# Gate weights spread by one broadcast DMA, strip 0 on ScalarE's queue, tile 3's transposes copied by ScalarE

## The chip, the cores and the metric

The kernel runs on one core of a Trainium2 chip. The metric is the device time of one execution in microseconds (us). The core has five engines with instruction queues of their own: TensorE (PE in the profile, its weight loads PEld), VectorE (DVE), ScalarE (ACT), GpSimd (POOL) and SyncE (SP, which here only issues DMAs). They wait for one another through semaphores. SyncE, ScalarE and GpSimd issue DMAs; all of these are moved by the same 16 DMA engines.

## The reference

Inputs are bfloat16: x of 2048 x 512 (one tensor of the two serves both branches), and weights.

```
g = sigmoid((x * gate_w).sum(-1))                 # one gate for each of the 2048 rows
a = attention(x, wqkv) @ wo                       # 32 heads of 16; each row sees 8 keys: itself and 2, 4, ... 14 rows back
h = layernorm(x)                                  # over the 512 features
u = gelu(h.T @ w1 + b1)                           # mixes the 2048 rows into 1792
y = (u @ w2 + b2).T                               # and back to 2048
out = g * a + (1 - g) * y
```

## The kernel before

All of the input fits in SBUF. x is held as 16 tiles of 128 rows by 512 features. The work is written as a list of operations with their reads, writes and guessed durations; a small planner (class _Sched) orders them for each engine by ready time and remaining path, and then every engine runs its list strictly in that order, with semaphore waits where one engine's operation needs another's. So an operation that waits holds up everything behind it on its engine.

The order on TensorE is: five warm-up products on constants (L568); transposes of x tiles 0 to 3 through PSUM (L586); the transposes of the two bias rows (L602, L603); one product that spreads the gate weights over the partitions (L643); four groups of "lead" products (L618), which begin the first layer of the token mixer for x tiles 0 to 3 as soon as each is normalised; the q, k and v projections (L713, 192 products); the rest of the mixer's first layer (L609), with the two score sums of the attention (L803, one for each half of the rows) put in between; and the second layer (L937) with the output projection of the attention (L946) behind it.

VectorE first takes the statistics of x tiles 0 to 3 (L623 and L627), and normalises each (L634) once ScalarE has made the reciprocal deviation with two small functions. It then computes the gate sums: for each x tile one multiply-and-reduce with the gate weights (L756, 16 in all, the tensor GWB of 128 x 512 holds the gate weights in every partition). Then come the products of queries with shifted keys for the attention (L468), which fill most of its time, with the statistics of the other tiles (L775) in between. The score sum of each half needs VectorE's last addition for that half.

How the gate weights get into GWB before the change: GpSimd clears a tensor of 128 x 512 (GWZ, L478), a DMA on ScalarE's queue puts the 1 KB of gate weights in its partition 0, TensorE multiplies it with a matrix of ones (L643, into PSUM bank 6), and ScalarE copies the product to GWB.

The transposes of x tiles 0 to 3 are copied from PSUM to the tensor XT, which the first projections read: those of tiles 0 to 2 by ScalarE (through the helper at L471), those of tile 3 by VectorE (L598). The bias transposes go to PSUM bank 7, beside tile 3's, and VectorE copies them (L674, L675).

The loads at the start are in a row on SyncE's queue, in the order in which they are written: x0, x1, x2, strip 0, x3, strips 1 to 3 (a strip is the part of w1 that the lead products of one tile use, 128 KB), the K weights in two parts, the first part of the Q weights, x4 and x5, the second Q weights, then transposing loads of x and the rest. ScalarE's queue has the two bias rows and the gate row. A load's operation waits only for its buffer; SyncE needs about 0.47 us for each issue.

Of the kernel before, what the change touches and what calls it, by code (L numbers as in the profile page):

```python
# [5 lines left out]
BF16 = mybir.dt.bfloat16  # L6
# [3 lines left out]
AF = mybir.ActivationFunctionType  # L10
# [3 lines left out]
D = 512  # L14
# [4 lines left out]
NST = S // 128  # L19
NFT = F // 128  # L20
# [8 lines left out]
NLEAD = 4  # L29
AVD = (1, 3, 5, 6)  # L30
GL = 4
# [259 lines left out]
class _Mem:  # L291
# [17 lines left out]
    def view(self, name, dtype, dims, extra=0, p0=0, np_=128):  # L309
        base = self.arena[:].bitcast(dtype)  # L310
        pst = base.ap[0][0]
        esz = mybir.dt.size(dtype)
        o = self.off[name]
        assert o % esz == 0
        return bass.AP(base.tensor, p0 * pst + o // esz + extra, [[pst, np_]] + [list(d) for d in dims])


def bass_gated_mix__sliding_local_dilated__mixer_token_mlp__prompt_kernel(nc, A_x, A_wqkv, A_wo, B_x, B_w1, B_b1, B_w2, B_b2, gate_w, out, dbg=None):
    with contextlib.ExitStack() as es:
# [49 lines left out]
        w1v = B_w1.rearrange("(st p) f -> p st f", p=128)  # L369
# [17 lines left out]
        W2ALIAS = [["w1s2"], ["w1s3"], ["w1s4"], ["p2"], ["w1s0"], ["w1s1"],  # L387
                   ["x%d" % t for t in range(7)], ["x%d" % t for t in range(7, 14)]]
        XTUSE = ["w1s3", "w1s4"]
        PR = [["p0", "p0b"], ["p1", "p1b"], ["p2", "p2h"], ["log0", "log1", "att0", "att1", "lw0", "lw1", "lw2", "lw3", "gwr"]]  # L390
        LW = view("LOG", BF16, [(128 * GL, NLEAD), (1, 128 * GL)])
        WO = view("WO", BF16, [(D, 4), (1, D)])
        QH = [view("Q%d" % h, BF16, [(HS, 4), (1, HS)]) for h in range(2)]
# [4 lines left out]
        LOG = [view("LOG", BF16, [(UT_, NW), (1, UT_)], extra=h * NW * UT_) for h in range(2)]  # L398
# [12 lines left out]
        E32 = view("E32", FP32, [(1, D)])  # L411
        GWB = view("GWB", BF16, [(1, D)])
        LX = view("LX", BF16, [(D, NLEAD), (1, D)])
        GWZ = view("LOG", BF16, [(1, D)], extra=NLEAD * 128 * GL)
        GW1 = psub(GWZ, 0, 1, 0, [(1, D)])
        JUNK = view("S4", BF16, [(D, 4), (1, D)])
        ZN = view("Z", FP32, [(1, 32)])
        TZ = view("Z", FP32, [(1, 32)], extra=32)
# [2 lines left out]
        IDENT = view("IDENT", BF16, [(1, 128)])  # L421
# [4 lines left out]
        B1R = view("ROWS", BF16, [(1, 128)], np_=NFT)  # L426
        B2R = view("ROWS", BF16, [(1, 128)], extra=128, np_=NST)
# [26 lines left out]
        B1C = small(NFT)  # L454
        B2C = small(NST)
# [5 lines left out]
        def psb(bank):  # L461
            return ps[:, bank, :].bitcast(BF16)
# [7 lines left out]
        def act(o_, i_, f_, **kw):  # L470
            return lambda e: e.activation(out=o_, in_=i_, func=f_, **kw)  # L471
# [3 lines left out]
        A("pool", lambda e: e.affine_select(out=IDENT, in_=ONES, pattern=[[1, 128]], compare_op=ALU.is_equal,  # L475
                                            fill=0.0, base=0, channel_multiplier=-1),
          0.4, reads=["ones"], writes=["ident"], name="ident")
        A("pool", lambda e: e.memset(GWZ, 0.0), 0.4, writes=["gwr"], name="gwz", prio=-50)  # L478
        A("pool", lambda e: e.memset(sub(KH[0], 0, [(KR, 4), (1, PAD)]), 0.0), 0.2, writes=["kpad"], name="kpad")  # L479
        A("pool", lambda e: e.memset(sub(V5, 0, [(VR, 4), (1, PAD)]), 0.0), 0.2, writes=["vpad"], name="vpad")  # L480

# [9 lines left out]

        last_ld = [None]

        def load(name, dst, src, nbytes, writes, transpose=False, queue="sp", issue=0.5, order=True, deps=(), reads=()):
            ds = sch.dsem(name)

            def fn(e):
                if transpose:
                    return e.dma_start_transpose(dst, src)
                return e.dma_start(dst, src)  # L500
            op = sch.dma(queue, fn, nbytes, ds, issue=issue, reads=reads, writes=writes, deps=deps,
                         after=([last_ld[0]] if order and last_ld[0] is not None else []), name=name)
            if order:
                last_ld[0] = op
            return op
# [11 lines left out]
        def ld_wq(name, d0, d1, res):  # L517
            load(name, WQKV[:, d0:d1, 0:D], wqkv_v[:, d0:d1, 0:D], (d1 - d0) * 128 * D * 2, [res], queue="act", order=False)

        def ld_strip(t, n):  # L520
            load("s%d" % t, LW[:, t:t + n, :], w1v[:, t:t + n, 0:128 * GL], n * 32768 * GL, ["lw%d" % t_ for t_ in range(t, t + n)])

        ld_x(0, 1)
        ld_x(1, 1)
        ld_x(2, 1)
        ld_strip(0, 1)
        ld_x(3, 1)
        ld_strip(1, 1)
        ld_strip(2, 1)
        ld_strip(3, 1)  # L530
        ld_w("wk01", 1, 0, 2, "wk")
        ld_w("wk23", 1, 2, 4, "wk2")
        load("gw", GW1, bass.AP(gate_w.tensor, gate_w.offset, [[D, 1], [1, D]]), 1024, ["gwr"], issue=0.4, queue="act", order=False)
        load("b1", B1R, B_b1.rearrange("(t p) -> t p", p=128), 4096, ["b1r"], issue=0.4, queue="act", order=False)
        load("b2", B2R, B_b2.rearrange("(t p) -> t p", p=128), 4096, ["b2r"], issue=0.4, queue="act", order=False)
        ld_w("wq01", 0, 0, 2, "wq")
        ld_x(4, 2)
        ld_w("wq23", 0, 2, 4, "wq2")
# [22 lines left out]
        WONE = nc.const_aps.tensor(1.0, [128, 128], BF16)  # L561
        WROW = nc.const_aps.tensor(1.0, [128, 512], BF16)

        def f_warm(n, bank):
# [4 lines left out]
                return ins  # L569
            return fn  # L570

        chain = [None]

        def PE(fn, dur, reads, writes, name, prio=0):
            op = A("pe", fn, dur, reads=reads, writes=writes, after=([chain[0]] if chain[0] is not None else []), name=name, prio=prio)
            chain[0] = op
            return op
# [12 lines left out]
        def tx(t):  # L590
            PE(f_tx(t), 0.4, ["x%d" % t, "ident"], ["b%d" % TXB[t][0]], "tx%d" % t)

        def ext(t, eng, after):
            bank, o = TXB[t]
            src = sub(psb(bank), o, [(128, 4), (1, 128)])
            dst = sub(XT, t * 128, [(S, 4), (1, 128)])
            if eng == "dve":
                return A("dve", lambda e: e.tensor_copy(out=dst, in_=src), 0.42, reads=["b%d" % bank], writes=["xt0_%d" % t], after=after, name="ext%d" % t, prio=-30)  # L598
            return A("act", act(dst, src, AF.Copy), 0.6, reads=["b%d" % bank], writes=["xt0_%d" % t], after=after, name="ext%d" % t, prio=-30)

        def f_tb(e):
            e.transpose(out=psb(7)[:, 512:512 + NFT], in_=B1R, identity=IDENT[0:NFT, 0:NFT])  # L602
            return e.transpose(out=psb(7)[:, 544:544 + NST], in_=B2R, identity=IDENT[0:NST, 0:NST])  # L603

        def f_ph2(ft, bank, s0, s1):
            def fn(e):
# [22 lines left out]
        def rstd(t, after=()):  # L629
            A("act", act(col(SD, t), AG[:, t, 1:2], AF.Ln, bias=1e-5), 0.25, reads=["ag%d" % t], writes=["sd%d" % t], after=after, name="lnl%d" % t, prio=-40)  # L630
            return A("act", act(col(RSTD, t), col(SD, t), AF.Exp, scale=-0.5), 0.25, reads=["sd%d" % t], writes=["rstd%d" % t], name="rs%d" % t, prio=-40)

        def apply(t, after):
            return A("dve", (lambda t_: lambda e: e.tensor_scalar(out=LX[:, t_, :], in0=X[:, t_, :], scalar1=AG[:, t_, 0:1], scalar2=col(RSTD, t_),  # L634
                                                                  op0=ALU.subtract, op1=ALU.mult))(t), 0.41, reads=["rstd%d" % t, "st%d" % t, "x%d" % t],
                     writes=["lx%d" % t], after=after, name="ln%d" % t, prio=-40)

        PE(f_warm(5, 0), 2.1, [], ["b0"], "warm0")
        tx(0)
        tx(1)  # L640
        PE(f_tb, 0.2, ["b1r", "b2r", "ident"], ["b7"], "t_b12")
        tx(2)
        PE(lambda e: e.matmul(ps[:, 6, :], lhsT=WONE, rhs=GWZ, start=True, stop=True), 0.4, ["gwr"], ["b6"], "gwbc")  # L643
        def lead(t):
            PE(f_lead(t), 0.87, ["lx%d" % t, "lw%d" % t], ["b%d" % ft for ft in range(GL)], "lead%d" % t)

# [1 line left out]
        ag = aggr(0)  # L648
# [3 lines left out]
        e0 = ext(0, "act", [r0])  # L652
        lead(0)
        ag = aggr(1, [l0])
        r1 = rstd(1)
        ew = A("act", act(GWB, ps[:, 6, :], AF.Copy), 0.6, reads=["b6"], writes=["gwb"], after=[r1], name="evgw", prio=-50)
        tx(3)
        s2 = stat(2, [ag])
        l1 = apply(1, [s2])
        lead(1)  # L660
        ag = aggr(2, [l1])
        r2 = rstd(2)
        s3 = stat(3, [ag])
        l2 = apply(2, [s3])
        ag = aggr(3, [l2])
        e1 = ext(1, "act", [r2, e0])
        r3 = rstd(3, [e1])
        ext(2, "act", [r3])
        e3 = ext(3, "dve", [ag])
        l3 = apply(3, [e3])  # L670
        e3 = l3
        lead(2)
        lead(3)
        A("dve", lambda e: e.tensor_copy(out=B1C, in_=psb(7)[:, 512:512 + NFT]), 0.15, reads=["b7"], writes=["b1c"], after=[e3], name="b1c", prio=-20)  # L674
        A("dve", lambda e: e.tensor_copy(out=B2C, in_=psb(7)[:, 544:544 + NST]), 0.15, reads=["b7"], writes=["b2c"], after=[e3], name="b2c", prio=-20)  # L675

        def f_rp(e):
            with nc.allow_low_precision(reason="exact 0/1 indicator sums"):
# [53 lines left out]
        for dl in range(4):  # L732
# [3 lines left out]
          reads=["k%d_1" % dl for dl in range(4)], writes=["khalo"], name="khalo")  # L736
# [18 lines left out]
        for t in range(NST):  # L755
            A("dve", (lambda t_: lambda e: e.tensor_tensor_reduce(out=JUNK[:, t_ % 4, :], in0=X[:, t_, :], in1=GWB, scale=1.0, scalar=0.0, op0=ALU.mult, op1=ALU.add,  # L756
                                                                  accum_out=col(Z, t_)))(t), 0.61, reads=["x%d" % t, "gwb", "s4"], writes=["z%d" % t, "jk%d" % (t % 4)], after=[e3],
              name="z%d" % t, prio=-4, delay=1.0 if t in (6, 7) else 0.0)
# [15 lines left out]
        for t in range(NLEAD, NST):  # L774
            A("dve", (lambda t_: lambda e: e.bn_stats(out=ST6[:, t_, :], in_=X[:, t_, :]))(t), 0.6,  # L775
              reads=["x%d" % t], writes=["st%d" % t], after=[e3], name="st%d" % t, prio=-4, delay=1.0 if t in (4, 5, 6, 7) else 0.0)
# [7 lines left out]
          reads=["md"], writes=["vv"], name="ln_var", prio=-20)  # L784
# [294 lines left out]
```

## Time and profile before

| what | us |
|---|---|
| median of three runs | 164.03 (163.46 to 165.6) |
| the profiled execution, its own time | 162.99 |
| its span, first to last instruction | 161.7 |
| TensorE busy | 158.7 |
| VectorE busy | 150.9 |
| ScalarE busy | 77.5 |
| GpSimd busy | 27.2 |
| first lead product starts | 4.82 |
| first projection starts | 8.72 |
| first gate sum starts | 7.86 |
| first long VectorE product of the attention starts | 14.29 |
| score sum of half 0 starts, of half 1 | 56.29, 91.05 |

Each line of an instruction view has the start in us from the span's start, the duration in us, the engine, the line of the kernel, the operation and its shapes; in brackets stands how long the engine was idle before it and what ended that wait. A "q" behind the engine's name (SPq) is the queue of its DMA issues. Durations of TensorE products include the pipeline; the distance from one start to the next is what a product costs.

### The profile page before, as it was taken

What the parts mean: (1) busy time and instruction counts of PE and PEld (TensorE: products, weight loads), DVE (VectorE), ACT (ScalarE), POOL (GpSimd) and SP (SyncE); (2) the same over time, 40 slices, a digit from 0 to 9 for tenths busy, and PEclk for the clock granted to TensorE, in tenths of its full rate; (3) what the DMA queues carried; (4) which work ended last, traced back from release to release, by engine and by line L of the source; (5) the groups of instructions that cost most, each with busy time, mean ns of one, the idle gap of its engine ahead of it and who ended that gap; (6) DMA issues with size and microseconds to landing.
All of it is one profiled execution on the core that took longest, in us unless ns stands there. A gap on an engine that the chain in (4) does not pass through costs nothing.

```text
span 161.7 us, 2009 instructions
## 1 busy us (share of the span) xinstructions
PE 158.7 (98%) x778; PEld 75.9 (47%) x778; DVE 150.9 (93%) x143; ACT 77.5 (48%) x103; POOL 27.2 (17%) x63
## 2 busy tenths in 40 slices
PE   7999999999999999999999999999999999999994
PEld 3455555555554444444444444444444444444652
DVE  2969999999999999999999999999999999999943
ACT  3827666679999381999311344420111111111153
POOL 4000011000000001200792030008580003020000
DMA  4899999999924999999399999999999913949504
GB/s 133 260 228 267 190 295 292 252 212 216 321 92 111 308 292 245 163 296 190 78 321 360 336 298 294 214 311 290 344 206 214 199 50 78 186 109 211 134 32 162
DMA packets 45303, 35.54 MB, mean 220 GB/s; under 512 B 8045, under 2 KB 42094, under 8 KB 45294
## 3 DMA queue, kind: packets, MB, share of 16 engines
q1 hardware_dynamic: 41392, 22.75, 53.4%
q0 software_dynamic: 3696, 12.59, 36.3%
q8 instruction: 6, 0.10, 0.2%
q10 hardware_dynamic: 206, 0.08, 0.2%
q14 instruction: 3, 0.02, 0.0%
HBM read 19.15 MB, written 2.11 MB: 131 GB/s over the span
## 4 chain that ended last, share of the span: by engine, by line
PE 98%; DVE 0%; issue 0%
PE ps L937 30%; PE ps L609 28%; PE ps L713 26%; PE ps L946 9%; PE ps L618 2%; PE ps L568 1%; PE ps L803 1%; PE ps L586 1%; DVE arena L955 0%; PE ps L643 0%; PE ps L602 0%; PE ps L603 0%
## 5 line engine op out<-in xcount | busy, mean ns | idle before, releaser
L468 DVE TENSOR_TENSOR arena<-arena 128x4096 bf16<-128x4096 bf16 (+6 forms) x71 | 125.7, 1807 | 1.5 <-DMA arena<-arena 0.3
L937 PE MATMUL ps<-arena 128*128 128x512 bf16 (+2 forms) x238 | 50.2, 366 | 0.0
L471 ACT ACTIVATE arena<-ps,arena 128x512 bf16<-128x512 f32 (+1 forms) x29 | 20.9, 727 | 55.5 <-PE ps L946 40.6
L609 PE MATMUL ps<-arena 128*128 128x512 bf16 x208 | 45.4, 379 | 0.0
L713 PE MATMUL ps<-arena 128*128 128x512 bf16 x192 | 41.6, 379 | 0.0
L471 ACT ACTIVATE arena<-ps 128x512 bf16<-128x512 f32 (+3 forms) x38 | 31.5, 843 | 14.4 <-PE ps L713 11.2
L937 PEld LDWEIGHTS ps<-arena 128*128 128x128 bf16 x238 | 23.3, 98 | 25.4
L609 PEld LDWEIGHTS ps<-arena 128*128 128x128 bf16 x208 | 20.2, 98 | 24.9 <-issue 0.8
L713 PEld LDWEIGHTS ps<-arena 128*128 128x128 bf16 x192 | 21.7, 113 | 19.7
L880 POOL DMA_DIRECT2D arena<-arena x32 | 17.1, 664 | 23.1 <-DVE arena L468 14.0
L471 ACT ACTIVATE arena<-arena 128x512 bf16<-128x512 bf16 (+6 forms) x27 | 15.2, 565 | 10.1 <-DVE arena L468 9.2
L946 PE MATMUL ps<-arena 128*128 128x512 bf16 (+2 forms) x68 | 15.6, 366 | 0.0
L831 POOL DMA_DIRECT2D arena<-arena x3 | 3.8, 1270 | 62.3 <-DVE arena L468 62.3
L1028 ACT ACT_TABLE_LOAD x9 | 11.5, 1283 | 2.3 <-POOL arena L479 2.2
L756 DVE CUSTOM_DVE_ANT_0 arena<-arena 128x512 bf16<-128x512 bf16 x16 | 10.2, 688 | 1.3 <-DMA arena<-in_A_x_dram 1.3
L901 POOL DMA_DIRECT2D arena<-arena x4 | 4.9, 1226 | 31.4 <-DVE arena L468 31.4
L946 PEld LDWEIGHTS ps<-arena 128*128 128x128 bf16 x68 | 6.6, 98 | 7.2
L775 DVE BATCH_NORM_STATS2 arena<-arena 128x6 f32<-128x512 bf16 x12 | 7.3, 677 | 0.0
L623 DVE BATCH_NORM_STATS2 arena<-arena 128x6 f32<-128x512 bf16 x4 | 2.7, 669 | 2.9 <-DMA arena<-in_A_x_dram 2.9
L955 DVE TENSOR_SCALAR arena<-ps,arena 128x512 bf16<-128x512 f32 (+1 forms) x2 | 1.3, 660 | 3.1 <-PE ps L946 3.0
L618 PE MATMUL ps<-arena 128*128 128x512 bf16 x16 | 4.0, 381 | 0.0
L568 PE MATMUL ps<-const-bfloat16-1.0 128*128 128x512 bf16 x5 | 2.3, 624 | 0.8 <-PEq L1064 0.8
(39 smaller groups left out, 19.0 us busy)
## 6 DMA issues: line engine op xcount, KB each, us to landing
arena<-in_B_w_dram SPq DMA_DIRECT2D x8, 896.0 KB, 13.3
arena<-arena POOLq DMA_DIRECT2D x6, 1024.0 KB, 9.2
arena<-in_B_w_dram SPq DMA_DIRECT2D x5, 1024.0 KB, 8.8
arena<-arena POOLq DMA_DIRECT2D x32, 128.0 KB, 7.3
arena<-arena POOLq DMA_DIRECT2D x1, 2048.0 KB, 17.9
out_dram<-arena SPq DMA_DIRECT2D x15, 128.0 KB, 2.6
arena<-in_B_w_dram SPq DMA_DIRECT2D x2, 768.0 KB, 13.6
arena<-in_A_wqkv_dram SPq DMA_DIRECT2D x4, 256.0 KB, 5.2
```

Source lines behind the costliest of these rows:

```text
L468: return lambda e: e.tensor_tensor(out=o_, in0=a_, in1=b_, op=op_)
L471: return lambda e: e.activation(out=o_, in_=i_, func=f_, **kw)
L609: ins = e.matmul(ps[:, bank, :], lhsT=W1S[W1AT[ft // 2]][:, st, 128 * (ft % 2):128 * (ft % 2) + 128], rhs=(LX if st < NLEAD else X)[:, st, :],
L618: ins = e.matmul(ps[:, ft, :], lhsT=LW[:, t, 128 * ft:128 * ft + 128], rhs=LX[:, t, :], start=(t == 0), stop=False)
L713: ins = e.matmul(ps[:, bank, :], lhsT=sub(WQKV, dt * 3 * D + tn * D + dl, [(4, 128)]), rhs=XT[:, dt, sb * 512:(sb + 1) * 512], start=(dt = ...
L756: A("dve", (lambda t_: lambda e: e.tensor_tensor_reduce(out=JUNK[:, t_ % 4, :], in0=X[:, t_, :], in1=GWB, scale=1.0, scalar=0.0, op0=ALU.m ...
L775: A("dve", (lambda t_: lambda e: e.bn_stats(out=ST6[:, t_, :], in_=X[:, t_, :]))(t), 0.6, reads=["x%d" % t], writes=["st%d" % t], after=[e ...
L880: prev = sch.dma("pool", (lambda d_, s_: lambda e: e.dma_start(d_, s_))(dst, src), 131072, ds, issue=1.0, reads=["att%d" % h], writes=["av ...
L901: sch.dma("pool", (lambda d_, s_: lambda e: e.dma_start(d_, s_, accum_op=ALU.add, max_dma_last_dim=4096))(sub(PB[b], 0, [(2048, 2), (1, 20 ...
L937: ins = e.matmul(ps[:, bank, 0:c1 - c0], lhsT=W2S[i // 2][:, ft, 128 * (i % 2):128 * (i % 2) + 128], rhs=UT[:, ft, c0:c1], start=(ft == 0) ...
L946: ins = e.matmul(ps[:, bank, 0:c1 - c0], lhsT=OT[:, i // 2, dl, 128 * (i % 2):128 * (i % 2) + 128], rhs=WO[:, dl, c0:c1], start=False, sto ...
L1028: e.preload_act_table_set(want)
```

## The change

Three things are changed together.

The gate weights are loaded straight into GWB: one DMA on SyncE's queue reads the same 1 KB of gate_w for each of the 128 partitions, 128 KB written. The cleared tensor, its memset, the product on TensorE and the copy on ScalarE are gone. The load stands behind the K weights and ahead of the first Q weights.

Strip 0 is loaded by ScalarE's queue, behind the two bias rows; x3 and strips 1 to 3 follow x2 directly on SyncE.

Tile 3's transposes are copied by ScalarE, so that tiles 1, 2 and 3 are copied there in turn, each one slot earlier than before. The bias transposes go to bank 6, which the gate product has left. Two small products of 128 columns on constants (f_fill) are put before the transposes of tiles 1 and 2.

The lists of the engines are otherwise in the same order as before.

```diff
@@ operands and GpSimd's start
-        GWZ = view("LOG", BF16, [(1, D)], extra=NLEAD * 128 * GL)
-        GW1 = psub(GWZ, 0, 1, 0, [(1, D)])
...
-        A("pool", lambda e: e.memset(GWZ, 0.0), 0.4, writes=["gwr"], name="gwz", prio=-50)
@@ loads
-        def ld_strip(t, n):
-            load("s%d" % t, LW[:, t:t + n, :], w1v[:, t:t + n, 0:128 * GL], n * 32768 * GL, ["lw%d" % t_ for t_ in range(t, t + n)])
+        def ld_strip(t, queue="sp", after=()):
+            return load("s%d" % t, LW[:, t, :], w1v[:, t, 0:128 * GL], 32768 * GL, ["lw%d" % t], queue=queue, order=queue == "sp", after=after)
 
         ld_x(0, 1)
         ld_x(1, 1)
         ld_x(2, 1)
-        ld_strip(0, 1)
         ld_x(3, 1)
-        ld_strip(1, 1)
-        ld_strip(2, 1)
-        ld_strip(3, 1)
+        for t in range(1, NLEAD):
+            ld_strip(t)
         ld_w("wk01", 1, 0, 2, "wk")
         ld_w("wk23", 1, 2, 4, "wk2")
-        load("gw", GW1, bass.AP(gate_w.tensor, gate_w.offset, [[D, 1], [1, D]]), 1024, ["gwr"], issue=0.4, queue="act", order=False)
-        load("b1", B1R, B_b1.rearrange("(t p) -> t p", p=128), 4096, ["b1r"], issue=0.4, queue="act", order=False)
-        load("b2", B2R, B_b2.rearrange("(t p) -> t p", p=128), 4096, ["b2r"], issue=0.4, queue="act", order=False)
+        load("gw", GWB, bass.AP(gate_w.tensor, gate_w.offset, [[0, 128], [1, D]]), 131072, ["gwb"])
+        prv = [load("b1", B1R, B_b1.rearrange("(t p) -> t p", p=128), 4096, ["b1r"], issue=0.5, queue="act", order=False)]
+        prv = [load("b2", B2R, B_b2.rearrange("(t p) -> t p", p=128), 4096, ["b2r"], issue=0.5, queue="act", order=False, after=prv)]
+        prv = [ld_strip(0, queue="act", after=prv)]
         ld_w("wq01", 0, 0, 2, "wq")
@@ TensorE's start
+        def f_fill(n, bank):
+            return lambda e: e.matmul(ps[:, bank, 0:n], lhsT=WONE, rhs=WROW[:, 0:n], start=True, stop=True)
...
         PE(f_warm(5, 0), 2.1, [], ["b0"], "warm0")
         tx(0)
+        PE(f_fill(128, 0), 0.1, [], ["b0"], "fill0")
         tx(1)
-        PE(f_tb, 0.2, ["b1r", "b2r", "ident"], ["b7"], "t_b12")
+        PE(f_tb, 0.2, ["b1r", "b2r", "ident"], ["b6"], "t_b12")
+        PE(f_fill(128, 0), 0.1, [], ["b0"], "fill1")
         tx(2)
-        PE(lambda e: e.matmul(ps[:, 6, :], lhsT=WONE, rhs=GWZ, start=True, stop=True), 0.4, ["gwr"], ["b6"], "gwbc")
@@ the copies
-        ew = A("act", act(GWB, ps[:, 6, :], AF.Copy), 0.6, reads=["b6"], writes=["gwb"], after=[r1], name="evgw", prio=-50)
...
-        r2 = rstd(2)
+        e1 = ext(1, "act", [r1, e0])
+        r2 = rstd(2, [e1])
...
-        e1 = ext(1, "act", [r2, e0])
-        r3 = rstd(3, [e1])
-        ext(2, "act", [r3])
-        e3 = ext(3, "dve", [ag])
-        l3 = apply(3, [e3])
+        e2 = ext(2, "act", [r2])
+        r3 = rstd(3, [e2])
+        ext(3, "act", [r3])
+        l3 = apply(3, [ag])
```

More of the change, by code (lines that the diff above doesn't have):

```diff
@@ L389, in bass_gated_mix__sliding_local_dilated__mixer_token_mlp__prompt_kernel @@
         XTUSE = ["w1s3", "w1s4"]
-        PR = [["p0", "p0b"], ["p1", "p1b"], ["p2", "p2h"], ["log0", "log1", "att0", "att1", "lw0", "lw1", "lw2", "lw3", "gwr"]]
+        PR = [["p0", "p0b"], ["p1", "p1b"], ["p2", "p2h"], ["log0", "log1", "att0", "att1", "lw0", "lw1", "lw2", "lw3"]]
         LW = view("LOG", BF16, [(128 * GL, NLEAD), (1, 128 * GL)])
@@ L492, in bass_gated_mix__sliding_local_dilated__mixer_token_mlp__prompt_kernel, with load @@
         last_ld = [None]
-        def load(name, dst, src, nbytes, writes, transpose=False, queue="sp", issue=0.5, order=True, deps=(), reads=()):
+        def load(name, dst, src, nbytes, writes, transpose=False, queue="sp", issue=0.5, order=True, deps=(), reads=(), after=()):
             ds = sch.dsem(name)
@@ L501, in load @@
             op = sch.dma(queue, fn, nbytes, ds, issue=issue, reads=reads, writes=writes, deps=deps,
-                         after=([last_ld[0]] if order and last_ld[0] is not None else []), name=name)
+                         after=list(after) + ([last_ld[0]] if order and last_ld[0] is not None else []), name=name)
             if order:
@@ L601, in f_tb @@
         def f_tb(e):
-            e.transpose(out=psb(7)[:, 512:512 + NFT], in_=B1R, identity=IDENT[0:NFT, 0:NFT])
-            return e.transpose(out=psb(7)[:, 544:544 + NST], in_=B2R, identity=IDENT[0:NST, 0:NST])
+            e.transpose(out=psb(6)[:, 512:512 + NFT], in_=B1R, identity=IDENT[0:NFT, 0:NFT])
+            return e.transpose(out=psb(6)[:, 544:544 + NST], in_=B2R, identity=IDENT[0:NST, 0:NST])
         def f_ph2(ft, bank, s0, s1):
@@ L673, in bass_gated_mix__sliding_local_dilated__mixer_token_mlp__prompt_kernel @@
         lead(3)
-        A("dve", lambda e: e.tensor_copy(out=B1C, in_=psb(7)[:, 512:512 + NFT]), 0.15, reads=["b7"], writes=["b1c"], after=[e3], name="b1c", prio=-20)
-        A("dve", lambda e: e.tensor_copy(out=B2C, in_=psb(7)[:, 544:544 + NST]), 0.15, reads=["b7"], writes=["b2c"], after=[e3], name="b2c", prio=-20)
+        A("dve", lambda e: e.tensor_copy(out=B1C, in_=psb(6)[:, 512:512 + NFT]), 0.15, reads=["b6"], writes=["b1c"], after=[e3], name="b1c", prio=-20)
+        A("dve", lambda e: e.tensor_copy(out=B2C, in_=psb(6)[:, 544:544 + NST]), 0.15, reads=["b6"], writes=["b2c"], after=[e3], name="b2c", prio=-20)
         def f_rp(e):
```

## The prediction

> **What bounds the kernel now.** I read the busy shares first, then the chain that ended last, then the first 16 us engine by engine, and last the DMA landings and the two places where TensorE takes a result of VectorE.
>
> The first part and the chain of the page:
>
> ```profile
> PE 158.7 (98%) x778; PEld 75.9 (47%) x778; DVE 150.9 (93%) x143; ACT 77.5 (48%) x103; POOL 27.2 (17%) x63
> ...
> PE 98%; DVE 0%; issue 0%
> ```
>
> TensorE is the whole chain: from 0.84 us on it hardly waits, and a product of 512 columns follows the last after 0.216 us (192 of them in 41.44 us in the chain). So nothing behind about 9 us can be gained here; only a wait of TensorE can be added or removed. VectorE is nearly as full, and its slack against TensorE is what decides.
>
> TensorE in the first 9 us (start, duration, what):
>
> ```profile
> 2.50 0.63 PE L568 MATMUL ps<-const-bfloat16-1.0 128*128 128x512 bf16 x1
> 3.04 1.12 PE L586 MATMUL ps<-arena 128*128 128x128 bf16 x8
> 4.24 0.53 PE L586 MATMUL ps<-arena 128*128 128x128 bf16 x4
> 4.60 0.38 PE L643 MATMUL ps<-arena,const-bfloat16-1.0 128*128 128x512 bf16 x1
> 4.82 1.03 PE L618 MATMUL ps<-arena 128*128 128x512 bf16 x4
> ```
>
> and what its weight loads wait for there:
>
> ```profile
> 4.81 0.55 PEld L618 LDWEIGHTS ps<-arena 128*128 128x128 bf16 x4 [0.16 <-DVE arena L634]
> 6.83 0.55 PEld L618 LDWEIGHTS ps<-arena 128*128 128x128 bf16 x4 [0.39 <-DVE arena L634]
> 7.84 0.55 PEld L618 LDWEIGHTS ps<-arena 128*128 128x128 bf16 x4 [0.46 <-DVE arena L634]
> ```
>
> The four lead products (L618) wait for the normalised tiles (L634) of VectorE. This stage runs at the pace of the chain statistics, aggregate, ScalarE's two small functions, apply; TensorE has idle time in it.
>
> VectorE between the normalised tiles and the first long product of the attention:
>
> ```profile
> 7.86 0.68 DVE L756 CUSTOM_DVE_ANT_0 arena<-arena 128x512 bf16<-128x512 bf16 x1
> ...
> 10.31 0.08 DVE L756 DVE_READ_ACCUMULATOR2_ANT arena<- 128x1 f32 x1
> 11.66 0.69 DVE L756 CUSTOM_DVE_ANT_0 arena<-arena 128x512 bf16<-128x512 bf16 x1 [1.27 <-DMA arena<-in_A_x_dram]
> ...
> 14.29 2.29 DVE L468 TENSOR_TENSOR arena<-arena 128x4096 bf16<-128x4096 bf16 x1
> ```
>
> Four gate sums run from 7.86 to 10.31, then 1.27 us of idling until x4 is there; from 11.66 to the first sum of the scores VectorE has no gap over 0.04 us.
>
> **The change, part by part.**
>
> *TensorE.* Removed: the gate product (L643), 0.216 us of array time at 4.60. Added: two fillers of 128 columns, each a quarter of a 512-column step, 0.11 us at the early step of 0.43 (the warm-up's weight loads start at 1.22, 1.65, 2.08). One lies in the hole before x1's transposes (3.42 to 3.55), one before x2's at 4.24. The first lead product was released by VectorE at 4.81, so the removal is worth nothing; the fillers may push the transposes by 0.1 us, which TensorE's holes of 0.05 and 0.14 us before the third and fourth lead products take up. Value 0; bounds -0.1 and +0.1.
>
> *ScalarE.* The copy of the gate row (0.58 us at 5.22) goes; tile 3's transpose copy comes (0.58 us, the same form as its siblings at 4.22, 6.23 and 7.24). The four slots stay, each with the next tile in it, and the last still ends at 7.82, before TensorE's first projection at 8.72: 0. The issue of strip 0 (about 0.43 us, as on SyncE) takes the place of the gate row's (0.28), so the table load moves from 2.18 to about 2.3 and ends at 3.6; its first user starts at 3.87: 0.
>
> *VectorE.* Tile 3's copy (0.39 us at 6.78) goes. It lay in the wait for ScalarE: the last apply starts at 7.37 after ScalarE's function ends at 7.33. Worth 0. Losing the cover costs nothing, for nothing else moves into that hole.
>
> *GpSimd.* A memset of 0.53 us ahead of the identity goes. The identity was ready by 1.83, and its first user follows the warm-up at 3.04: 0.
>
> *The loads.* On SyncE strip 0 leaves the row, so x3, strips 1 to 3 and the two K weight loads each go out one slot (0.47 us) earlier; the gate load takes the slot at 5.04, and all behind it keep their slots. The bytes ahead of the last K weights stay as they were, 1.5 MB, and the engines are nearly full (DMA share 0.83 to 0.96 in every microsecond from 2 to 10), so I take their landing as unchanged within 0.4 us. The slot in question, with SyncE's time of issue and time to landing:
>
> ```profile
> 5.04 0.47 SPq L500 DMA_DIRECT2D arena<-in_A_wqkv_dram  x1
> ```
>
> ```profile
> arena<-in_A_wqkv_dram SPq DMA_DIRECT2D x1, 256.0 KB, 5.2
> ```
>
> Before, the last K weights went out there and landed at 10.2. The spread gate row is 128 KB behind the same 1.5 MB. Its price has no row of its own: from below, 128 KB at the 264 to 274 GB/s of 8 to 10 us is 0.48 us, less up to 0.4 us for the earlier issue; from above, the four loads that spread the gate's logs (64 KB each, one row to 32 partitions) moved 127 to 137 GB/s, paced by their issues, which makes 1.0 us. I take +0.25: landing at 10.45, between 10.0 and 11.2.
>
> Here is the added wait. The first gate sum is now behind that landing, and everything on VectorE is queued behind it. The gate sums start at about 10.55 instead of 7.86; four take 2.45 us, to 13.0. x4, pushed by the gate row from 11.5 to some 12.0, is there by then, so the fifth starts at 13.0 instead of 11.66. **VectorE is 1.34 us late**, and with no gap left it carries that to the scores. What that meets:
>
> ```profile
> 50.98 4.43 DVE L468 TENSOR_TENSOR arena<-arena 128x8192 bf16<-128x8192 bf16 x1
> ...
> 56.29 1.05 PE L803 MATMUL ps<-arena 128*32 128x512 bf16 x16
> ```
>
> VectorE's last sum of half 0 ends at 55.41, and TensorE's score product starts at 56.29. Less 0.06 us from VectorE's end to TensorE's start (6.77 to 6.83 above) that is a slack of 0.82. 1.34 - 0.82 = **0.52 us of waiting on TensorE** before L803. After it TensorE too is 0.52 late, which covers the rest: half 1's sum ends at 89.65 for a product at 91.05 (slack 1.34), the last attention tile at 155.70 for its product at 156.82 (slack 1.06).
>
> *The other landings.* The second Q weights move from 12.26 to about 12.7 for a use at 13.03 (8.72 + 20 x 0.216); the first from 10.85 to 11.3 for 12.17. Strip 0 now shares the engines with x1 to x3: by about 4.6 the same bytes are in. Value 0, upper end 0.3.
>
> The Trainium skill, DMA: Bandwidth & Descriptors, section "Anatomy of one DMA — SWDGE (gpsimd) path", fits a transfer as 2.0 us plus its bytes at 436 GB/s. By that the gate row would take an estimated 2.3 us and land at 7.3, ahead of the first gate sum, and the sum would be no change. The trace's 128 KB loads issued from 1.7 to 2.7 us did land after 2.3 to 2.4 us; behind a full queue at 5.04 it was 5.2 us, and I go by that.
>
> **The sum**: 162.99 us (the profiled execution: span 161.7 and 1.3 around it) + 0.52 = 163.5. The three runs have a median 1.04 above the profiled one, so a median of the changed kernel should lie near **164.5**, 0.3% slower. A measurement of this kernel can hardly tell less than 2% (3.3 us) from no change.
>
> **The rivals.**
>
> *The wait is covered.* If the gate row lands by 9.9, the four sums end by 12.5, VectorE is at most 0.82 us late and L803 never waits: 162.99, a median of 164.0, not slower. The earlier issue of the K weights speaks for it, the full engines against. Chance 0.22. The landing at 7.3 by the Trainium skill's fit would belong here.
>
> *A slow spread.* 128 readers of one kilobyte of HBM may queue up. At half the rate of the 64 KB spreads (66 GB/s) the row takes 1.95 us and lands at 12.1; VectorE is 3.0 late, L803 waits 2.2 us: median 166.2. The Q weights behind it would then stall TensorE at 12 to 13 us by about 1 us, inside the same 2.2. Past 2% needs a landing after 13.2. Against it: most packets of the 64 KB spreads took 46 ns, as others do. Chance 0.13, of which 0.03 past 2%.
>
> *A late clock.* The transposes of x0 and x1 take 311 ns in the median, those of x3 219; the array doubles its pace near 4.5 us. If the new pattern, without the long product, moves that past the second lead product, two lead products take 1.73 instead of 0.87 us: 1.7 less 0.19 of idle, 165.5. The profile's granted clock reads 1.00 throughout and shows nothing of it. The Trainium skill, TensorE: Matmul & The Clock Gate, Part 1, says that the array runs at half pace until a free-running window of some 3.4 us has been busy; the fillers come before 4.5 us and the removed product after, which by that rule speaks against this rival. Chance 0.05.
>
> *Weights late.* The second K weights land at 10.21 for a use at 10.44. Noise of single packets (up to 1 us) can turn that 0.2 us into a wait of 0.5: 164.5 to 165. Chance 0.05.
>
> The forecast (gate row between 9.95 and 11.2) keeps 0.55.
>
> **The numbers.** Without a stall and on the profiled execution's scale 163.0 is the lower end; a stall of 2 us on the median's scale, 166.0, the upper. Faster by over 2% would need 3.3 us out of a chain without waits: 0.03. Slower by over 2%: the slow spread's 0.03 and as much for what I don't see: 0.06. Within 2%: 0.91.
>
> **What would show it.** VectorE idle from about 7.95 to 10.5, released by the gate load's DMA; no wait for x4; the first long product at about 15.6 instead of 14.29; L803 at about 56.8 with half a microsecond of TensorE waiting for VectorE; the lead products where they were. I am wrong if the gate row lands before 9.9 or after 11.2, or if TensorE's first projection leaves 8.72.

## The result, and the profile after

Over 22 runs each, taken in turn, the median is 164.41 us (163.36 to 166.06) with the change and 163.62 us (162.98 to 165.6) without it. The ratio is 1.0051 with a 95% interval of 1.0035 to 1.0066: half a percent slower, 0.8 us. The forecast was 164.5 us and 0.5 us of loss. Medians here and below are over all runs, while the ratios leave out those that lie more than 1.5% above the fastest run of their kernel (among them one of the 22 with the change, one of 12 with both edits undone, and three of 12 with a late x2).

The profiled execution took 165.29 us (span 164.0), one of the slower ones, and the page of its profile already says that it is another case than the one forecast as likeliest. Busy time, and the shares of the chain that ended last:

```profile
PE 160.5 (98%) x779; PEld 76.9 (47%) x779; DVE 150.7 (92%) x142; ACT 77.6 (47%) x103; POOL 26.7 (16%) x62
...
PE 96%; DMA 2%; SPq 0%; DVE 0%; issue 0%
```

The chain no longer starts on TensorE. It begins with a load of x, and 2% of 164 us is 3.3 us. TensorE is busy 1.8 us longer with the same products, so something ran at a slower pace. TensorE's timeline from the filler before x2 on (start, duration, line) shows what:

```profile
4.26 0.29 PE L569 MATMUL ps<-const-bfloat16-1.0 128*128 128x128 bf16 x1
5.05 0.61 PE L585 MATMUL ps<-arena 128*128 128x128 bf16 x4 [0.50 <-DMA arena<-in_A_x_dram]
5.45 1.91 PE L617 MATMUL ps<-arena 128*128 128x512 bf16 x4
7.16 0.63 PE L585 MATMUL ps<-arena 128*128 128x128 bf16 x4
7.59 3.60 PE L617 MATMUL ps<-arena 128*128 128x512 bf16 x12
11.02 1.24 PE L712 MATMUL ps<-arena 128*128 128x512 bf16 x5
```

Against the lines of before: x2's transposes start at 5.05 instead of 4.24, after a wait for x2's load; the four products of the first lead group take 1.91 us instead of 1.03, for they start every 0.43 us, not every 0.216; and the first projection comes at 11.02 instead of 8.72. TensorE has lost 2.3 us by then and loses no more. VectorE, in the same execution:

```profile
11.47 0.69 DVE L755 CUSTOM_DVE_ANT_0 arena<-arena 128x512 bf16<-128x512 bf16 x1 [3.23 <-DMA arena<-in_gate_w_dram]
```

The gate sums do wait for the gate row, as forecast, and longer than forecast: it was issued at 5.15 and landed at 11.45. VectorE's first long product starts at 16.60, 2.31 us later than before. But TensorE is 2.30 us late as well, so the score product at 58.60 finds the sum of 57.72 with the same 0.82 us to spare as before. In this execution the forecast wait happened and was hidden by a loss on the other engine. Two delays lie side by side, and one profile can't say which of them the median is made of.

### The profile page after: what moved, and what is told of

Its sections match the earlier page's. It is cut to its first block, busy times and chain, and to the rows that moved or that the text cites. A ratio compares the mean times of both kernels' runs of the same rounds, so it can differ in the third digit from the quotient of the medians.

```text
span 164.0 us, 2009 instructions
## 1 busy us (share of the span) xinstructions
PE 160.5 (98%) x779; PEld 76.9 (47%) x779; DVE 150.7 (92%) x142; ACT 77.6 (47%) x103; POOL 26.7 (16%) x62
## 4 chain that ended last, share of the span: by engine, by line
PE 96%; DMA 2%; SPq 0%; DVE 0%; issue 0%
PE ps L936 29%; PE ps L608 27%; PE ps L712 25%; PE ps L945 8%; PE ps L617 3%; DMA arena<-in_A_x_dram 2%; PE ps L802 1%; PE ps L585 1%; SPq L497 0%; DVE arena L954 0%
## 5 line engine op out<-in xcount | busy, mean ns | idle before, releaser
L608 PE MATMUL ps<-arena 128*128 128x512 bf16 x208 | 45.4, 379 | 0.0
L712 PE MATMUL ps<-arena 128*128 128x512 bf16 x192 | 41.6, 379 | 0.0
L945 PE MATMUL ps<-arena 128*128 128x512 bf16 (+2 forms) x68 | 15.6, 366 | 0.0
L617 PE MATMUL ps<-arena 128*128 128x512 bf16 x16 | 5.5, 503 | 0.0
```

The source lines that it names most:

```text
L608: ins = e.matmul(ps[:, bank, :], lhsT=W1S[W1AT[ft // 2]][:, st, 128 * (ft % 2):128 * (ft % 2) + 128], rhs=(LX if st < NLEAD else X)[:, st, :],
L617: ins = e.matmul(ps[:, ft, :], lhsT=LW[:, t, 128 * ft:128 * ft + 128], rhs=LX[:, t, :], start=(t == 0), stop=False)
L712: ins = e.matmul(ps[:, bank, :], lhsT=sub(WQKV, dt * 3 * D + tn * D + dl, [(4, 128)]), rhs=XT[:, dt, sb * 512:(sb + 1) * 512], start=(dt = ...
L945: ins = e.matmul(ps[:, bank, 0:c1 - c0], lhsT=OT[:, i // 2, dl, 128 * (i % 2):128 * (i % 2) + 128], rhs=WO[:, dl, c0:c1], start=False, sto ...
```

## The experiments

Three explanations were to be told apart. **Gate row**: VectorE waits for the gate row, and the score product for VectorE. **Strip**: strip 0, now beside x2 on the DMA engines, makes x2 late, and the hole on TensorE keeps the array at half pace. **Slow spread**: 128 reads of one kilobyte are slow by themselves, and delay the gate sums and every load behind them. Each run was compared with runs of the kernel before on the same chip: the first four on one, the next four on a second, the last three on a third. The planner orders the operations anew for every kernel, so in some of them small operations of VectorE stand in another place than before.

### The changed kernel once more

> The changed kernel unchanged, for a second profiled execution. Gate-row theory (the prediction): the first gate sum starts behind the gate row's landing at 10.5 to 11.5 us, and the score product of half 0 waits 0.5 to 1.4 us for VectorE if TensorE's lead stage ends near 8.7; ratio to before 1.003 to 1.008. Strip theory (the first profile: x2 landed at 5.00 instead of 4.01 because strip 0 shares the engines, and TensorE kept its slow pace until 9.1): x2 lands at 4.6 to 5.0 again, the first projection starts at 9 to 11 us instead of 8.72, and the score product does not wait.

The median is 164.54 us against 163.46 (12 and 35 runs), ratio 1.0073 (1.0043 to 1.0102). The profiled execution (163.55 us, span 162.3) shows the forecast case. VectorE:

```profile
10.65 0.69 DVE L755 CUSTOM_DVE_ANT_0 arena<-arena 128x512 bf16<-128x512 bf16 x1 [2.67 <-DMA arena<-in_gate_w_dram]
...
13.11 0.69 DVE L755 CUSTOM_DVE_ANT_0 arena<-arena 128x512 bf16<-128x512 bf16 x1
...
15.72 2.28 DVE L466 TENSOR_TENSOR arena<-arena 128x4096 bf16<-128x4096 bf16 x1
```

TensorE, at the first projection and at the score product of half 0:

```profile
8.76 0.81 PE L712 MATMUL ps<-arena 128*128 128x512 bf16 x3
```

```profile
56.87 1.05 PE L802 MATMUL ps<-arena 128*32 128x512 bf16 x16 [0.31 <-DVE arena L466]
```

The fifth gate sum no longer waits for x4; the first long product is 1.43 us late; the first projection is where it was (8.76 for 8.72); and the score product waits for VectorE. From first projection to score product it is 48.11 us here and 47.57 before: 0.54 us more. Of these, 0.38 us lie directly before the score product (0.69 us from the start of the product ahead of it, against 0.31 before), and 0.15 us earlier, at 23.6 us, where a weight load stood until a copy of ScalarE was done, by the profile. VectorE's sum ends at 56.82, so without the earlier wait the score product would have waited that much longer. (The bracket says 0.31 because it counts from a modelled end.) x2 landed at 4.10 this time, so the hole did not open. The changed kernel thus has at least two kinds of execution, and the two profiles hit one of each. But 163.55 us is among the three fastest of these 12 runs and 1.0 us under their median: this profile shows that the forecast wait exists, not what the median is made of.

### Strip 0 back on SyncE

```diff
         ld_x(2, 1)
+        ld_strip(0)
         ld_x(3, 1)
...
-        prv = [ld_strip(0, queue="act", after=prv)]
```

> Strip 0 back on SyncE between x2 and x3; the rest as changed, so that the gate row goes out one slot later (about 5.6 us). Strip theory: x2 lands near 4.0, the first projection starts at 8.7, the time is that of before (ratio 1.000 to 1.002). Gate-row theory: the first gate sum starts at 11 to 12 us, VectorE is 1.5 to 2.5 us late, the score product of half 0 waits 0.7 to 1.7 us, ratio 1.004 to 1.010.

163.71 us against 163.46, ratio 1.0027 (1.0002 to 1.0053): lower than the changed kernel's 1.0073, though the intervals overlap, and not quite the time of before. In the profile x2 landed at 4.01 and the first projection started at 8.65. The gate sums started at 10.13 behind a gate row that landed at 10.10, and VectorE's first long product at 14.99, 0.70 us late, within the slack of 0.82: the score product did not wait in this execution. Neither account is hit cleanly. The gate row came earlier here than expected, since the K weights ahead of it landed at 9.06 (10.22 and 9.40 in the two profiles before), and a small reduction of 0.28 us was moved ahead of the gate sums into the hole.

### No wait for the gate row

```diff
-            A("dve", (lambda t_: lambda e: e.tensor_tensor_reduce(out=JUNK[:, t_ % 4, :], in0=X[:, t_, :], in1=GWB, scale=1.0, scalar=0.0, op0=ALU.mult, op1=ALU.add,
-                                                                  accum_out=col(Z, t_)))(t), 0.61, reads=["x%d" % t, "gwb", "s4"], writes=["z%d" % t, "jk%d" % (t % 4)], after=[e3],
+            A("dve", (lambda t_: lambda e: e.tensor_tensor_reduce(out=JUNK[:, t_ % 4, :], in0=X[:, t_, :], in1=X[:, 0, :], scale=1.0, scalar=0.0, op0=ALU.mult, op1=ALU.add,
+                                                                  accum_out=col(Z, t_)))(t), 0.61, reads=["x%d" % t, "x0", "s4"], writes=["z%d" % t, "jk%d" % (t % 4)], after=[e3],
```

> The changed kernel with the gate load still issued, but the gate sums multiply with x tile 0 (in SBUF long before) instead of the gate row: the gates are other numbers, the work is the same, and VectorE no longer waits for the load. Gate-row theory: back to before (ratio 0.999 to 1.002), long products start at 14.3 to 14.8 us. Strip theory: the loss of TensorE's lead stage stays, ratio 1.003 to 1.008.

163.67 us against 163.46, ratio 1.0020 (0.9995 to 1.0045). By the ratio most of the loss is gone with the wait; the profile shows what can remain. VectorE:

```profile
13.12 0.69 DVE L755 CUSTOM_DVE_ANT_0 arena<-arena 128x512 bf16<-128x512 bf16 x1 [2.69 <-DMA arena<-in_A_x_dram]
```

The first four sums started at 7.90, as before. Then the fifth waited 2.69 us for x4, which stands behind the gate row in the queue and landed at 12.98 instead of 11.52. The long products started at 15.73, the same 1.4 us late as in the second profile of the changed kernel. So the wait of VectorE has a second source, which taking away the reader does not take away. In this execution (164.55 us, above the median of its 12) the score product did not wait for VectorE at all. TensorE itself lost 1.4 us between the first projection and the score product (49.01 us against 47.57): it stood for the two Q weights, which landed at 12.30 and 13.65 instead of 10.85 and 12.26, and at 25.0 us for a late load of x.

### Both undone

The two edits above together.

> Both at once: strip 0 back on SyncE and the gate sums with x tile 0 in place of the gate row. Every theory: the time of before, ratio 0.998 to 1.002. If either of the two single undos alone reaches that, it names the cause; if neither does and this one does, the two delays lie side by side and each hides the other.

164.09 us against 163.46, ratio 1.0030 (1.0004 to 1.0056). Every theory had it at the time of before, and it is not: the gate load is still issued, and in the profile it stood 2.1 us in the queue (K weights landed at 9.88, the gate row at 12.02), so that x4 came at 13.45 and VectorE waited 3.1 us for it. The time was lost on TensorE, though, in the projections:

```profile
12.90 1.03 PE L712 MATMUL ps<-arena 128*128 128x512 bf16 x4 [0.29 <-DMA arena<-in_A_wqkv_dram]
14.16 1.05 PE L712 MATMUL ps<-arena 128*128 128x512 bf16 x4 [0.24 <-DMA arena<-in_A_wqkv_dram]
```

The Q weights, next in the queue behind the row, landed at 12.76 and 14.12, and the two waits lengthen the way from first projection to score product by 0.9 us (48.46 against 47.57). With a first projection that is 0.27 us late (8.99) this is the whole 1.2 us by which the span is longer; the score product did not wait for VectorE. What these two undos left in place, the load itself, was worth looking at.

### The price of reading one row over and over

512 KB are put into the kernel before, between the K weights and the first Q weights, into a buffer that nobody reads: once as four copies of the gate row per partition, once as 512 rows of x. Both have 512 packets of 1 KB. Each was run once.

```diff
         ld_w("wk23", 1, 2, 4, "wk2")
+        load("probe", view("P1", BF16, [(D, 4), (1, D)]), bass.AP(gate_w.tensor, gate_w.offset, [[0, 128], [0, 4], [1, D]]), 524288, ["p1", "p1b"])
...
+        load("probe", view("P1", BF16, [(D, 4), (1, D)]), xv[:, 12:16, :], 524288, ["p1", "p1b"])
```

> The kernel before with one load more on SyncE between the K weights and the first Q weights: four copies of the gate row for each of the 128 partitions (512 KB, every packet the same kilobyte of HBM) into a buffer that nothing reads. In the two profiles so far 128 KB of this kind took 1.0 to 2.1 us between the landings before and behind it. Slow-spread theory: 512 KB take 4 us or more from the landing of the last K weights to its own. Bulk theory (bytes alone): 1.8 to 2.2 us, as 256 KB behind it take 0.65 to 0.75 us each.

> The same with 512 KB of distinct rows (x tiles 12 to 15) in place of the copies of one row; as many packets of 1 KB. Slow-spread theory: 1.3 to 2.2 us from the last K weights to its landing, well under half of what the copies take. Bulk theory: the same as the copies.

Issue on SyncE, size and time to landing of the copies, and what the core moved in three of its microseconds (the last columns are the granted clock, the DMA engines' share and GB/s):

```profile
5.55 0.47 SPq L500 DMA_DIRECT2D arena<-in_gate_w_dram  x1
```

```profile
arena<-in_gate_w_dram SPq DMA_DIRECT2D x1, 512.0 KB, 10.2
```

```profile
9.00:10.00 1.00, 1.00 (x7) 0.48 (x5) 1.00 (x5) 0.00 (x0) 0.00 (x0) 1.00 0.76 109
10.00:11.00 1.00, 0.99 (x5) 0.53 (x5) 0.56 (x3) 0.00 (x0) 0.00 (x0) 1.00 0.60 63
11.00:12.00 1.00, 0.96 (x5) 0.55 (x5) 0.00 (x0) 0.76 (x2) 0.00 (x0) 1.00 0.73 102
```

And of the distinct rows:

```profile
arena<-in_A_x_dram SPq DMA_DIRECT2D x1, 512.0 KB, 5.9
```

```profile
9.00:10.00 1.00, 1.00 (x6) 0.55 (x5) 1.00 (x5) 0.00 (x0) 0.00 (x0) 1.00 0.84 218
10.00:11.00 1.00, 0.95 (x6) 0.52 (x5) 0.53 (x3) 0.00 (x0) 0.00 (x0) 1.00 0.92 250
11.00:12.00 1.00, 1.00 (x5) 0.50 (x5) 0.00 (x0) 0.87 (x2) 0.00 (x0) 1.00 1.06 354
```

The copies landed at 15.74, 6.59 us behind the K weights (9.15): 80 GB/s. The distinct rows landed at 11.46, 1.64 us behind the K weights (9.82): 320 GB/s. In the three microseconds shown the whole core moves 63 to 109 GB/s with the copies (152 to 164 in the next three) and 218 to 354 with the rows, and what is queued behind the copies comes late: x4 landed at 17.16, against 12.89 behind the rows. The run with the copies took 169.42 us, with TensorE standing 4.1 us before the first Q weights; the one with distinct rows took 163.57 us, where before had 163.41. Four times the single gate row's 1.0 to 2.1 us makes 4.2 to 8.6 us, and the 6.6 us lie within it: the row's price fits that of the copies, not that of the bytes. The two loads also read different tensors. A load that repeats one row of x would have told repetition from the place in HBM; it was not run.

The run with the copies shows one thing more. The products after that stand come every 0.43 us from 17.9 to 21.2 us, and here the granted clock (the third column from the end) says why:

```profile
18.00:19.00 1.00, 1.00 (x3) 0.33 (x3) 1.00 (x4) 0.03 (x1) 0.00 (x0) 0.50 1.28 290
```

So a step of 0.43 us is a clock of one half, and here the clock fell about a microsecond after TensorE had stood for 4.1 us.

### No gate load at all

The kernel with both undone, and without the gate load; of the change only the copies on ScalarE, the missing gate product and the fillers are left.

```diff
-        load("gw", GWB, bass.AP(gate_w.tensor, gate_w.offset, [[0, 128], [1, D]]), 131072, ["gwb"])
```

> Strip 0 back on SyncE, no gate load at all, gate sums with x tile 0 (gates are other numbers, the same work): of the change only the copies on ScalarE, the missing gate product and the fillers are left. If these cost nothing, as the prediction has it: ratio 0.998 to 1.001, x4 lands near 11.5 again. If the two undos of e4 left a loss because of the fillers or copies: 1.002 to 1.005 as there.

163.35 us against 163.41, ratio 0.9995 (0.9982 to 1.0007). x4 landed at 11.12. So the copies, the removed product and the fillers cost and gain nothing that the 12 runs show (0.3 us at most by the interval), and the loss lies in the loads. It also answers whether another place for this load could beat the kernel before: without any load the time is only equal, so that was not tried.

### The same load from distinct rows

```diff
-        load("gw", GWB, bass.AP(gate_w.tensor, gate_w.offset, [[0, 128], [1, D]]), 131072, ["gwb"])
+        load("gw", GWB, xv[:, 15, :], 131072, ["gwb"])
```

> The changed kernel with the gate load reading 128 distinct rows (x tile 15) in place of one row 128 times: the same bytes, packets, slot and wait (the gates are other numbers). Slow-spread theory: the load lands 0.3 to 0.6 us behind the K weights in place of 1.0 to 2.1, the gate sums start at 9.8 to 10.5, the score product waits less than 0.3 us, ratio 1.000 to 1.004. Bulk theory: as the changed kernel, 1.005 to 1.008.

163.37 us against 163.41, ratio 0.9999 (0.9978 to 1.0021). Slot, bytes, packets, wait and the strip on ScalarE's queue are those of the change; only the source is another, and the half percent is gone: the upper end of the interval lies below the 1.0035 and 1.0043 at which those of the changed kernel begin, though that kernel was not run beside this one. In its profile the load landed 0.74 us behind the K weights, more than the 0.3 to 0.6 expected, and the gate sums started at 9.28, earlier than the expected 9.8, because the K weights themselves landed at 8.52, the earliest of all profiles.

That profiled execution itself took 165.17 us, the only one of 12 above 164, and shows the other delay without the gate row's. TensorE:

```profile
5.08 0.61 PE L585 MATMUL ps<-arena 128*128 128x128 bf16 x4 [0.63 <-DMA arena<-in_A_x_dram]
5.48 1.91 PE L617 MATMUL ps<-arena 128*128 128x512 bf16 x4
...
10.89 1.46 PE L712 MATMUL ps<-arena 128*128 128x512 bf16 x6
```

x2 landed at 5.04, and the array kept half pace until about 9: the picture of the first profile after the change.

### Strip 0 alone on ScalarE's queue

```diff
         ld_x(2, 1)
-        ld_strip(0, 1)
         ld_x(3, 1)
...
+        ld_strip(0, 1, queue="act", order=False)
```

> The kernel before with strip 0 alone moved to ScalarE's queue (behind the two bias rows and the gate row); gate product and copies as before. If the strip move is free in the median, as the plain-rows run has it: ratio 0.998 to 1.002, with perhaps 1 to 3 of 12 runs above 165 us, where x2 comes late. Strip theory in its strong form (the move costs by itself): 1.003 or more, x2 landing at 4.5 to 5.0 in the profile.

163.44 us against 163.21, ratio 1.0015 (0.9998 to 1.0032), none of 12 runs above 164.4. In the profile x2 landed at 4.21 and the first projection started at 8.98. In the median the move costs 0.2 us, and by the interval 0.5 us at most. That it makes x2 late enough for half pace shows in two profiles of other kernels, not in this run.

### A late x2, and the hole filled

Strips 0 and 1 are put ahead of x2 in the kernel before:

```diff
-        ld_x(2, 1)
         ld_strip(0, 1)
+        ld_strip(1, 1)
+        ld_x(2, 1)
         ld_x(3, 1)
-        ld_strip(1, 1)
```

In a second kernel two products on constants are put before x2's transposes as well:

```diff
+        PE(f_warm(2, 0), 0.85, [], ["b0"], "fill1")
         tx(2)
```

> The kernel before with strips 0 and 1 loaded ahead of x2, so that x2 lands near 5.1 us in every run and TensorE stands idle from 4.2 to 5.1. Clock theory (an idle hole before 4.5 us keeps the array at half pace for another 3 to 5 us): first projection at 10.0 to 11.2 us, 1.3 to 2.5 us more than before, ratio 1.008 to 1.015. Landing theory (only the late tile costs): VectorE's chain is 0.4 us late, the first projection starts at 9.1 to 9.3, ratio 1.001 to 1.004.

> The same with two products of 512 columns on constants put before x2's transposes (0.85 us at the early pace), which keep TensorE at work until x2 is there. Clock theory: the array doubles its pace near 4.5 to 5.5 us again, the first projection starts at 9.0 to 9.4, ratio 1.001 to 1.005 and below the unfilled one by 0.5% or more. Landing theory: as the unfilled one or up to 0.2 us more.

With the hole open the 12 runs fall into two groups, five from 163.31 to 163.78 and seven from 165.05 to 166.05; the median is 165.17 against 163.21. The ratio is 1.0063 (1.0030 to 1.0095), that of the medians 1.012, within the clock theory's range. The profile is from the upper group, with a first projection even later than that theory had it:

```profile
5.13 0.61 PE L586 MATMUL ps<-arena 128*128 128x128 bf16 x4 [0.88 <-DMA arena<-in_A_x_dram]
...
5.96 1.91 PE L618 MATMUL ps<-arena 128*128 128x512 bf16 x4
...
11.48 0.81 PE L713 MATMUL ps<-arena 128*128 128x512 bf16 x3
```

With the hole filled there is one group, 163.56 to 164.39, median 163.88, ratio 1.0037 (1.0021 to 1.0053):

```profile
4.19 0.61 PE L568 MATMUL ps<-const-bfloat16-1.0 128*128 128x512 bf16 x2
5.22 0.40 PE L586 MATMUL ps<-arena 128*128 128x128 bf16 x4 [0.42 <-DMA arena<-in_A_x_dram]
...
5.67 1.03 PE L618 MATMUL ps<-arena 128*128 128x512 bf16 x4
...
9.35 2.97 PE L714 MATMUL ps<-arena 128*128 128x512 bf16 x12
```

x2 is as late in both (5.09 and 5.18). More constant work on TensorE makes the kernel 1.3 us faster in the median: the slower group is gone in ten of ten runs. That these were the executions at half pace is shown by one profile and otherwise argued from the times. The profile with the hole filled can't show what the filler does, for in it the array had doubled its pace at about 4.1 us, before the two constant products, which follow each other after 0.23 us. The 0.7 us that are left against before are lost ahead of the first projection (9.35 against 8.72; from there to the score product it is 47.57 us in both). That the late tile on VectorE's chain is the reason is argued only.

## Why the prediction was right, and where it was not

The added wait, the step on which the forecast stood, is shown in the second profile: the first gate sum is released by the gate row, the fifth no longer waits for x4, VectorE is late, and the score product of half 0 pays what exceeds 0.82 us. VectorE is 1.43 us late there (forecast 1.34), the long products start at 15.72 (15.6), the score product at 56.87 (56.8), 0.54 us later against the first projection (0.52). The run with distinct rows shows the cause of the loss in the median: with the same wait on a fast load it is gone. The first profile has both of the signs by which the forecast was to be called wrong: the row landed at 11.45, and the first projection left 8.72.

That the numbers are so near is in good part luck. The row landed near the forecast (10.63 for 10.45) because the K weights came 0.81 us sooner than in the profile of the kernel before (9.40 for 10.21) while the row came 1.23 us behind them instead of 0.25. And the median of 164.41 us hits the forecast 164.5 because two errors cancel: the median without the change is 0.63 us above its profiled execution over 22 runs, where three runs had made it 1.04, and the loss is 0.79 us instead of 0.52.

The steps priced at nothing, TensorE's product and fillers, ScalarE's slots, VectorE's copy and GpSimd's memset, cost nothing that shows: 0.9995 without the loads.

The term that was mis-sized is the price of the spread. The forecast took it from bytes and from the spreads of 64 KB, 0.48 to 1.0 us, and put the landing between 10.0 and 11.2. It is 1.0 to 2.1 us in the five profiles that have it, and landings run from 10.10 to 12.02, three of the five past 11.2. It also delays the loads behind it more than forecast: x4 came at 11.97 to 13.45 where about 12.0 was expected, and the second Q weights at 12.66 to 14.12 where it was 12.7. So the step that gave these other landings a value of 0, 0.3 at most, failed as well: in two of the five profiles TensorE stood 0.5 and 0.9 us for the Q weights, with no wait for VectorE at all. The rival that named the slow reads had a chance of 0.13, and it named this stall too. How much of the median's loss goes through VectorE and how much through the Q weights is not shown.

Another step failed in some executions: "strip 0 now shares the engines with x1 to x3: by about 4.6 the same bytes are in". x2 landed at 4.10, 4.21, 4.28, 5.00 and 5.04 in the five profiles with strip 0 on ScalarE's queue, against 4.01 to 4.33 in the others that keep x2's place. In the first profile x2 and strip 0, issued at 1.72 and 1.85, landed at 5.00 and 5.20. The Trainium skill, DMA: Bandwidth & Descriptors, section "Queues, rings and completion order", says that each DMA engine takes turns between the queues that have work for it; the two profiles with the late x2 agree, with 0.2 us between the two landings. In the other three they lie 0.34 to 0.60 us apart, which is no less than on one queue (0.35 to 0.81 us), so what makes x2 late in some executions only is not shown.

The late clock was a rival at 0.05, with 165.5 us as its time and the removed product as its reason. The time was right (165.29 in the profile), by luck, for the rival had 1.5 us of loss on the scale of the median and the profile has 2.3 us on its own; and the reason was wrong: what keeps the array at half pace is the hole before x2's transposes, which the fillers of 128 columns are too short to fill. I had weighed those fillers as speaking against this case. The Trainium skill, TensorE: Matmul & The Clock Gate, Part 1, has a free-running window of some 3.4 us that must be busy before the array gets its full pace. The traces agree: with x2 in time the steps fall to 0.216 us somewhere between 4 and 6 us; with the hole at 9.1 to 9.8, which is 4.1 to 4.6 us after its end; the same kernel falls into two groups; and the half clock in the run with the copies lasted 3.4 us (17.7 to 21.1).

How much half-pace executions take stays open, but if 165 us parts them from the others, it is the smaller part of the median's 0.8 to 1.1 us. Of 34 runs of the changed kernel 8 took more than 165 us, of 107 runs of the kernel before 2, and one of 12 in each of the two runs with strip 0 back on SyncE, so such times are not the strip's alone. The medians of the changed kernel's other runs are 164.27 and 164.46 us, still 0.7 and 1.0 us above before. Putting strip 0 back took 0.0046 off the ratio in one comparison, moving it alone added 0.0015 in another, and with a fast gate load it cost nothing in the median: the intervals are too wide to split the sum further.

## What to carry to other kernels

A broadcast by DMA is not free bytes: price it by a spread in the trace that reads as few rows, or measure it, and put it behind the loads that somebody waits for (by argument; no such place was tried here). Where two engines both run without gaps, look for a delay on each: a loss on one hides the wait that a loss on the other causes, and one execution pays only the larger. Look at several executions before a profile is called typical. In the first microseconds a load that comes half a microsecond late can cost two if TensorE idles meanwhile; constant products as long as the possible hole are cheap.

## What was not expected of the hardware

In one run each, reading one kilobyte of HBM 512 times went at 80 GB/s, reading 512 different kilobytes in the same slot at 320 GB/s, and during the former the core as a whole moved as little as 63 GB/s, with 16 DMA engines at a share of 0.60.

Less than a microsecond of idling at the start can decide the pace of the array: with 0.9 us of hole seven of 12 executions were over 1.2 us slower than the other five, and the profiled one of these kept half pace to 9.7 us; with 0.4 us of hole behind constant work none of ten was. The granted clock reads 1.00 throughout both of these profiles, also where the products come every 0.43 us. Only in the run with the copies, where the clock fell in the middle, does the profile show it, as 0.50.
